# A memory-attention and GEGLU kernel: probabilities kept in two tiles, G evicted ahead of a nested addition, nested pieces in another order

## The chip, the cores and the metric

The kernel runs on one core of one Trainium2 chip. The metric is the device time of one execution in microseconds; what is given for a kernel is the median of its runs. Matmuls run on TensorE (PE; its weight loads are shown as PEld), the other work on VectorE (DVE), ScalarE (ACT) and GpSimd (POOL), and DMAs are issued by SyncE (SP).

## The reference

One sequence of 2048 rows, width 576, goes through two branches, and a sigmoid gate mixes them:

```python
q, k, v = x @ wq, x @ wk, x @ wv          # 32 heads of 18, 4 segments of 512 rows
for s in range(4):                        # per head
    p = softmax(qs @ ks.T * 18**-0.5 + causal_mask)
    a_dot = p @ vs
    a_mem = (phi(qs) @ M) / (phi(qs) @ z + 1e-6)     # phi(t) = t + 1 if t > 0 else exp(t)
    o = sigmoid(beta) * a_mem + (1 - sigmoid(beta)) * a_dot
    M, z = M + phi(ks).T @ vs, z + sum(phi(ks))
a = o @ wo
b = (gelu(x @ w_gate) * (x @ w_up)) @ w_down         # width 4608 inside
out = g * a + (1 - g) * b                 # g = sigmoid(sum(x * gate_w))
```

All is float32. The kernel keeps each matmul operand as two 16-bit words, a high one (the rounded value) and a low one (what the rounding left), and takes three products for one: high by high, high by low, low by high. A pair is made in two instructions: ScalarE copies to 16 bits, and Pool or VectorE subtracts.

## The kernel before

The program has three parts. First the four segments are projected (`project`, `put_columns`, `put_rows`), with the memory M and its recall; the loop runs over segments s and eight tiles j, and small pieces of other work are hung in by `beside_rows`, `behind_rows`, `beside_products`. Then come 72 steps `step(v)` of the inner width: v is split into f, p (block of 128 inner columns, half of the rows) and into fb, i4 (pair of blocks, place within it). Each makes two outputs of 128 inner columns by 512 rows twice (gate and up), in a scheme with fewer products than the plain one (Strassen's kind): sums of x and sums of weights are formed ahead, and three banks of the matmuls' memory, G (`X`), U (`Y`) and V, gather the products. The products of V are themselves nested one level deeper for half of the steps: `nest(at, n)` with n from 0 to 3 runs in the steps with i4 == 3 and i4 == 0, for the step behind, and piece 4 at the start of that step. Between the pieces VectorE copies or adds half a bank (`hold`, 256 columns). At the end VectorE multiplies gate and up (`hidden`), ScalarE and Pool make the pair (`hidden_pair`), and the down-projection of a block that is done runs as `chains` of `down` pieces, six matmuls of 288 columns in a "dn" bank each, which VectorE adds to `acc`. The third part is the output projection.

Attention lies inside the steps. With LAG 4, step v handles head index k = v - 4, a head of one half of the rows, in two units a = 2k and 2k + 1 (one segment each). For a unit, `scores` issues four matmuls (128, 256, 384 and 512 columns); `piece(qi)` lets VectorE add the mask, write the piece to the tile pf and find its maxima; `powers` has ScalarE form the bound mb and four exponentials; `pair_rows` makes the pairs of 768 and 512 columns (ScalarE's copy to ph, L1136, Pool's subtraction into pf itself, L1137); `turn_rows` turns ph and pf by DMA (L1142) into pt; `values` multiplies pt with the values. The tile pf has two buffers. The banks of the pieces are "st" (two) and "dn" (two, shared with the down-projection) and "pv".

The order of the work is written by hand: in `step` each engine takes its instructions in the order of the calls, and nothing is reordered. What is hung in where is decided by lines like these, near the start of a step and at its end:

```python
            weights_nest(fb, i4, 0)
...
            if on(k - 1):
                powers(2 * k - 1)
                pair_rows(2 * k - 1, 0)
                pair_rows(2 * k - 1, 1)
                turn_rows(2 * k - 1)
...
            nest(at, 3)
            ends.append((f, e, Y, g1))
```

`weights_nest` and `weights_first` scale, sum and pair the next blocks' weights (`nest_pairs`, L375 on ScalarE and L377 on Pool; `nest_sums`, L384 to L387 on Pool; `low_g`, L342). `scale_g` (L304, VectorE) scales a block of raw weights. `result_low` (L1186, VectorE) makes the low words of an attention result once in four steps.

Of the kernel before, what the change touches and what calls it, by code (L numbers as in the profile page):

```python
# [13 lines left out]
OP = mybir.AluOpType  # L14
# [29 lines left out]
def kernel(ctx: ExitStack, tc: tile.TileContext, xs, wqk, wv, wo, wgu, wd, beta, out):  # L44
# [475 lines left out]

    first, stay = ExitStack(), ctx.enter_context(ExitStack())
    with tc.tile_pool(name="prj", bufs=2, side="right", reuse_waits="tile") as pp:
# [45 lines left out]
        def make_v(k):  # L568
            t = W[9 + k] = pa.tile([P, 2, D + 2], F16, name="wv", bufs=5)
            pair_of(t, raw_v[:, k], wsc[:, 1:2])  # L570
# [186 lines left out]
        with tc.manual_schedule(engines=ORDERED):  # L757
# [96 lines left out]
            def beside_rows(s, q):  # L854
# [14 lines left out]
                if s == 3 and q == 1:  # L869
                    scales(0)  # L870
                    scales_out(0)
                    scale_g(0)
                    scale_g(1)

            def behind_rows(s, q):
                if s == 3:
                    if q < 3:
                        form_sums(1, q, -1, pool if q == 0 else dve)
                    if q == 0:
                        squares(0, 0, 0, act_square)  # L880
                    if q == 3:
                        rescale_words(2)
                        high_g(0, 0)
                        low_g(0, 0)

            def beside_products(s, j):
                if 0 < s < 3 and j == XJ[s]:
                    scale_x(s + 1)
                if s == 0:
# [31 lines left out]
                    if 3 <= j < 6:  # L921
                        finish_later()
                    if 1 <= j < 6:
                        make_v(j - 1)
                    if j == XJ[0]:
                        norm_x(0, bank("V"))
                        scale_x(1)
# [110 lines left out]
            put_columns(*done)  # L1038
            recall(3, 3)
            finish_later()  # L1040
# [10 lines left out]
    with tc.tile_pool(name="keep", bufs=2, side="right", reuse_waits="tile") as kp, ExitStack() as tail:  # L1051
# [3 lines left out]
        pairs16, turned_p, pvb = {}, {}, {}  # L1055
# [40 lines left out]
        COL = [0, P, 3 * P, 6 * P, 10 * P]  # L1096

        PIECES = ((3, 0, "st", "st"), (2, 64, "st", "st"), (1, 64, "dn", "dn"), (0, 0, "pv", "dn"))

        def scores(a):  # L1100
# [4 lines left out]
            prob[a] = ap_.tile([P, 10 * P], F32, name="pf", bufs=2)  # L1105
# [6 lines left out]
            def piece(qi):  # L1112
                dve.tensor_tensor_reduce(prob[a][:, COL[qi] : COL[qi + 1]], out[qi], mask[:, L - (qi + 1) * P :],  # L1113
# [4 lines left out]
        def powers(a):  # L1118

            p = prob[a]  # L1120
            b = ap_.tile([P, 4], F32, name="mb", bufs=2)
            c = 2 * (a // (2 * H)) + a % 2
            act.activation(b, mx.pop(a), AF.Copy, bias=LN256, scale=esc[:, 1, c : c + 1])  # L1123
            for qi in (1, 0, 2, 3):
                r = p[:, COL[qi] : COL[qi + 1]]
                act.activation(r, r, AF.Exp, bias=b[:, qi : qi + 1], scale=esc[:, 0, c : c + 1])  # L1126

        def pair_rows(a, i):

            p = prob[a]  # L1130
            if i == 0:
                pairs16[a] = ap_.tile([P, 10 * P], F16, name="ph", bufs=2)
                turned_p[a] = ap_.tile([P, 20, P], F16, name="pt", bufs=2)
            h = pairs16[a]
            cols = (slice(0, 6 * P), slice(6 * P, 10 * P))[i]
            act.activation(h[:, cols], p[:, cols], AF.Copy)  # L1136
            pool.tensor_tensor(p.bitcast(F16)[:, cols], p[:, cols], h[:, cols], OP.subtract)  # L1137

        def turn_rows(a):
            t = turned_p[a]  # L1140
            for i, h in enumerate((pairs16.pop(a), prob.pop(a).bitcast(F16)[:, : 10 * P])):
                sp.dma_start(t[:, 10 * i : 10 * i + 10], h, transpose=True)  # L1142
# [94 lines left out]
        def gl_tile():  # L1237
            return mp2.tile([P, L], F32, name="gl", bufs=3)

        def product(o, f, a, x, h, l, start=False):  # L1240

            w = pair_g[f]
            for k in range(2):
                for i, b in ((0, h), (0, l), (1, h)):
                    pe.matmul(o, w[:, i, (a + k) * P : (a + k + 1) * P], x[:, b + k],  # L1245
                              start=start and k == 0 and i == 0 and b == h, stop=k == 1 and i == 1,
                              skip_group_check=True)

# [69 lines left out]
        ahead = {}  # L1318

        def first_product(v):  # L1320
            f, p = divmod(v, 2)
            V = bank("V")
            w = flat(s3_first["t"])
            for k, b in ((0, X00), (1, X10)):
                for i, j in ((0, 0), (0, 1), (1, 0)):
                    a = (4 * i + 2 * f + k) * P
                    x = nest_x(p)[j][:, b * HX : (b + 2) * HX]
                    pe.matmul(V, w[:, a : a + P], x, start=k == i == j == 0, stop=k == i == 1, skip_group_check=True)
            if v == 3:
                s3_first.pop("t")  # L1330
                hh_free.append(s3_first.pop("slot"))
            g1 = gl_tile()
            dve.tensor_copy(g1, V)
            return V, g1

# [8 lines left out]
        def nest(at, n):  # L1344
# [24 lines left out]
            if n == 4:  # L1369
                nest_product(b, A, WS4, X11, p)  # L1370

        ends, puts = [], {}

        def end_pair():

            for g in ends:
                hidden(*g)
                if g is ends[0]:
# [3 lines left out]
            for f, c, o, g in ends:  # L1382
# [3 lines left out]
        def step(v):  # L1386
# [22 lines left out]
            elif i4 < 2:  # L1409
                if on(k - 2):  # L1410
                    values(2 * k - 3)
                nest((fb, p), 4)
                V, g1 = nested.pop((fb, p)), gl_tile()
                dve.tensor_copy(g1, V)
# [5 lines left out]
            put(2 * k - 1, 3)  # L1420
            dve.tensor_copy(Y, X)
            if v == 0:
                last_sum(1, 1)
                nest_sums_x(0)
            if v == 1:
                nest_sums_x(1)
            if v in (2, 3):
                for i in range(2):
                    nest_pairs_x(v - 2, i)
# [381 lines left out]
```

## Time and profile before

| | |
|---|---|
| median of 3 runs | 1620.98 us (1614.13 to 1621.68) |
| profiled execution | 1622.97 us |
| its span, from the first to the last instruction | 1621.3 us |
| mean granted TensorE clock | 0.996 |
| TensorE busy, 0 to 219 us (projections) | 211.75 us |
| TensorE busy, 219 to 290 us (first steps) | 66.00 us, clock 0.95 |
| TensorE busy, 290 to 1500 us (steps with attention) | 1182.66 of 1210 us |
| TensorE busy, 1500 to 1622 us (the tail) | 116.93 us |

In the rows of a timeline the first number is the start in us from the span's start, the second the time of the merged instructions, then engine, line, operation, output<-inputs, shapes and count; brackets give how long the engine sat idle before, and who released it. In rows of waits stand the total in us, the number of times and the longest. In a row of a window stand its bounds, its length, the busy time and instruction count of PE, PEld, DVE, ACT and POOL, the granted clock, the DMA share and GB/s. Ends of matmuls are modelled, so idle times on TensorE are a little less than the distance between starts shows.

### The profile page before, as it was taken

How to read it: one execution, taken by the hardware profiler on the slowest of the kernel's cores; microseconds unless marked ns; L12 is line 12 of the kernel's file. 1: busy time of each engine (PE TensorE's matmuls, PEld its weight loads, DVE VectorE, ACT ScalarE, POOL GpSimd, SP SyncE). 2: the span in 40 equal slices, each digit the busy share in tenths (PEclk: the TensorE clock that was granted, in tenths of full speed). 3: DMA queues.
4: the chain of work that ended last, by engine and by line, in shares of the span. 5: the costliest groups of instructions: out<-in, count | busy, mean ns of one | idle time of the engine just before them, and what ended most of it. 6: DMA issues, size and time to landing. Idle time of an engine off the chain costs nothing. (4 is left out here: it accounts for less than half of the span.)

```text
span 1621.3 us, 34060 instructions
## 1 busy us (share of the span) xinstructions
PE 1577.3 (97%) x12220; PEld 962.6 (59%) x12220; DVE 1272.2 (78%) x3256; ACT 1180.6 (73%) x2057; POOL 1119.6 (69%) x1218
## 2 busy tenths in 40 slices
PE   9999998999999999999999999999999989999999
PEld 5665654565556655555566565556555555656577
DVE  6779884878788878878787887788888878887665
ACT  7466543879788888878887877888888878786421
POOL 4245556677686867686867767686858676876597
PEclk9999999999999999999999999999999999999999
DMA  6533331567786787877777777778787878764546
GB/s 225 205 121 112 129 129 57 105 122 127 121 140 127 125 136 139 128 134 122 132 130 130 130 126 121 134 128 136 135 142 134 127 126 130 137 120 91 110 85 172
DMA packets 472834, 209.98 MB, mean 130 GB/s; under 512 B 427688, under 2 KB 437416, under 8 KB 472152
## 3 DMA queue, kind: packets, MB, share of 16 engines
q1 hardware_dynamic: 472664, 207.80, 66.3%
q8 instruction: 96, 1.57, 0.4%
q14 instruction: 74, 0.61, 0.1%
HBM read 91.87 MB, written 27.26 MB: 73 GB/s over the span
## 5 line engine op out<-in xcount | busy, mean ns | idle before, releaser
L1137 POOL TENSOR_TENSOR pf<-pf,ph 128x768 f16<-128x768 f32 (+1 forms) x256 | 366.5, 1432 | 305.4 <-ACT ph L1136 295.2
L1245 PEld LDWEIGHTS <-pairg 128*128 128x128 f16 x2592 | 251.3, 99 | 266.2 <-issue 26.9
L1203 PE MATMUL dn<-paird,hhr 128*128 128x288 f16 x2124 | 327.8, 287 | 6.8 <-DVE mx L1113 6.7
L1211 DVE SCALAR_TENSOR_TENSOR acc<-dn,ev,acc 128x288 f32<-128x288 f32 x534 | 271.4, 514 | 44.0 <-PE dn L1203 35.6
L1126 ACT ACTIVATE pf<-pf,mb,esc 128x256 f32<-128x256 f32 (+3 forms) x512 | 292.9, 642 | 5.5 <-issue 0.4
L1203 PEld LDWEIGHTS <-hhr 128*128 128x128 f16 x2160 | 207.3, 98 | 101.5 <-issue 20.9
L1245 PE MATMUL G<-x,pairg 128*128 128x512 f16 x864 | 211.2, 381 | 5.5 <-DVE gl L1226 5.5
L1245 PE MATMUL U<-xt,pairg 128*128 128x512 f16 x864 | 210.0, 379 | 1.6 <-DVE gl L1471 1.6
L1203 PE MATMUL dn<-paird,hhd 128*128 128x288 f16 x1272 | 205.3, 287 | 5.7 <-DVE mx L1113 5.7
L1136 ACT ACTIVATE ph<-pf 128x768 f16<-128x768 f32 (+1 forms) x256 | 172.4, 720 | 0.0
L342 POOL TENSOR_TENSOR pairg<-raw,pairg 128x384 f16<-128x384 f32 (+2 forms) x144 | 158.2, 1120 | 15.5 <-ACT pairg L338 15.5
L1203 PEld LDWEIGHTS <-hhd 128*128 128x128 f16 x1296 | 124.9, 98 | 58.1 <-issue 12.7
L1113 DVE CUSTOM_DVE_ANT_0 pf<-st,mask 128x512 f32<-128x512 f32 (+1 forms) x256 | 157.2, 614 | 0.0
L1113 DVE CUSTOM_DVE_ANT_0 pf<-dn,mask 128x256 f32<-128x256 f32 (+1 forms) x192 | 67.2, 375 | 99.1 <-PE dn L1110 61.8
L1123 ACT ACTIVATE mb<-mx,esc 128x4 f32<-128x4 f32 x128 | 37.1, 290 | 120.9 <-DVE mx L1113 120.8
L1235 ACT ACTIVATE gl<-gl,sc 128x512 f32<-128x512 f32 x110 | 75.2, 713 | 56.8 <-DVE gl L1498 40.8
L1341 PE MATMUL V<-xt,nest 128*128 128x256 f16 x714 | 106.4, 273 | 8.5 <-DVE hold L1368 3.7
L1245 PE MATMUL U<-x,pairg 128*128 128x512 f16 x432 | 106.2, 383 | 0.8 <-DVE gl L1498 0.8
L1245 PE MATMUL V<-x,pairg 128*128 128x512 f16 x432 | 106.5, 383 | 0.0
L1232 POOL TENSOR_TENSOR hhr<-gl,hhr 128x512 f16<-128x512 f32 x67 | 80.9, 1217 | 19.5 <-ACT hhr L1231 18.2
L1341 PEld LDWEIGHTS <-nest 128*128 128x128 f16 x714 | 66.5, 97 | 42.1 <-issue 24.5
L1156 PE MATMUL pv<-vt,pt 128*128 128x37 f16 x2560 | 85.2, 179 | 3.9 <-DMA pt<-pf 3.9
(355 smaller groups left out, 3128.5 us busy)
## 6 DMA issues: line engine op xcount, KB each, us to landing
raw<-in_wgu_dram SPq DMA_DIRECT2D x36, 640.0 KB
rawd<-in_wd_dram SPq DMA_DIRECT2D x36, 288.0 KB
qt<-qk SPq DMA_DIRECT2D x132, 72.0 KB
kt<-qk SPq DMA_DIRECT2D x132, 72.0 KB
qk<-stage SPq DMA_DIRECT2D x36, 256.0 KB
qt<-qk SPq DMA_DIRECT2D x132, 36.0 KB
kt<-qk SPq DMA_DIRECT2D x132, 36.0 KB
vp<-vstage SPq DMA_DIRECT2D x16, 296.0 KB
```

What stands on the lines that cost most here:

```text
L342: pool.tensor_tensor(spot(f, *p, 1), raw_g[f][:, p[0] : p[1]], spot(f, *p, 0), OP.subtract)
L1113: dve.tensor_tensor_reduce(prob[a][:, COL[qi] : COL[qi + 1]], out[qi], mask[:, L - (qi + 1) * P :], 1.0, -3e38, OP.add, OP.max, mx[a][:, q ...
L1126: act.activation(r, r, AF.Exp, bias=b[:, qi : qi + 1], scale=esc[:, 0, c : c + 1])
L1136: act.activation(h[:, cols], p[:, cols], AF.Copy)
L1137: pool.tensor_tensor(p.bitcast(F16)[:, cols], p[:, cols], h[:, cols], OP.subtract)
L1156: pe.matmul(ov, pr[:, 10 * i + COL[qi] // P + kb], v[:, 4 * e + kb, c0 : c0 + VC], start=kb == 0 and i == 0, stop=kb == qi and i == 1)
L1203: pe.matmul(o[:, :NH], hh[:, a, q * P : (q + 1) * P], w[:, b, n * NH : (n + 1) * NH], start=i == 0, stop=i == 5)
L1211: dve.scalar_tensor_tensor(av, o[:, :NH], ev, av, OP.mult, OP.add)
L1232: pool.tensor_tensor(hh[:, 1], t, hh[:, 0], OP.subtract)
L1235: act.activation(t, o, AF.Gelu_apprx_tanh, scale=scl[f // 2][0][:, 2 + c : 3 + c])
L1245: pe.matmul(o, w[:, i, (a + k) * P : (a + k + 1) * P], x[:, b + k], start=start and k == 0 and i == 0 and b == h, stop=k == 1 and i == 1, ...
L1341: pe.matmul(o, w[:, (7 * c + i) * P : (7 * c + i + 1) * P], x[d], start=start and n == 0, stop=n == 2, skip_group_check=True)
```

## The change

The tile pf is split in two: pb23 holds the pieces of 384 and 512 columns, pb01 those of 128 and 256. `pair_rows` and `turn_rows` are merged into `powers`; the pairs have 896 and 384 columns, and the low words of both go into pb23:

```diff
-        COL = [0, P, 3 * P, 6 * P, 10 * P]
+        COL = {2: 0, 3: 3 * P, 0: 7 * P, 1: 8 * P}
+        SPLIT = 7 * P
...
+            big = ap_.tile([P, SPLIT], F32, name="pb23", bufs=2)
+            prob[a] = big, ap_.tile([P, 10 * P - SPLIT], F32, name="pb01", bufs=2)
...
+            low = prob[a][0].bitcast(F16)
+            for i, (p, cols) in enumerate(zip(prob[a], (slice(0, SPLIT), slice(SPLIT, 10 * P)))):
+                for qi in ((3, 2), (1, 0))[i]:
+                    r = scored(a, qi)
+                    act.activation(r, r, AF.Exp, bias=b[:, qi : qi + 1], scale=esc[:, 0, c : c + 1])
+                act.activation(h[:, cols], p, AF.Copy)
+                pool.tensor_tensor(low[:, cols], p, h[:, cols], OP.subtract)
+            prob.pop(a)
+            for i, r in enumerate((h, low[:, : 10 * P])):
+                sp.dma_start(t[:, 10 * i : 10 * i + 10], r, transpose=True)
```

In a step, G is evicted by `hidden` before nested piece 3's addition (`end_first`), piece 4 (`nest_last`) comes behind product X, the copies of V and of G come ahead of a score piece, and `powers` of the odd unit comes ahead of `weights_nest`:

```diff
+            if fb and i4 < 2:
+                nest_last(fb, V, p)
+                dve.tensor_copy(g1, V)
+                dve.tensor_copy(Y, X)
+                put(2 * k - 1, 3)
...
-            weights_nest(fb, i4, 0)
...
             if on(k - 1):
                 powers(2 * k - 1)
-                pair_rows(2 * k - 1, 0)
-                pair_rows(2 * k - 1, 1)
-                turn_rows(2 * k - 1)
+            weights_nest(fb, i4, 0)
...
-            some(fb - 1, early[3:4])
+            some(fb - 1, early[3:])
             put(2 * k, 3)
-            some(fb - 1, early[4:])
...
+            if on(k - 1):
+                values(2 * k - 2)
+            if v != 3:
+                nest(at, 2)
             if low is not None:
                 result_low(low)
-            if on(k - 1):
-                values(2 * k - 2)
             if fb:
                 low_rests(f, (X, U4, x1), (Y, UG, x2_))
                 ends.append((f, c, X, g0))
+                if at:
+                    end_first()
```

In the first block, the nested pieces of v == 3 stand between its products and no longer in one run, `first_product(3)` uses the bank "pv", and some sums and scalings of x and of weights come later:

```diff
+            if v == 3:
+                nest(at, 0)
             some(fb - 1, early[0 if v == 4 else 1 : 2])
...
+            if v == 3:
+                nest(at, 1)
             some(fb - 1, early[2:3])
...
+            if v == 3:
+                nest(at, 2)
...
-            if v == 2:
-                scale_g(3, FRONT)
```

In the projections, `make_v(3)` and `make_v(4)` form their pairs on ScalarE and Pool, `scale_g(0)` and `scale_g(1)` are called from `behind_rows` and no longer from `beside_rows`, and segment 0 takes its `norm_x` and `scale_x` at another place:

```diff
+            if k < 3:
+                pair_of(t, r, sc)
+                return
+            act.activation(r, r, AF.Copy, scale=sc)
+            act.activation(t[:, 0], r, AF.Copy)
+            pool.tensor_tensor(t[:, 1], r, t[:, 0], OP.subtract)
...
-                    scale_g(0)
-                    scale_g(1)
...
+                    if 0 < q < 3:
+                        scale_g(q - 1)
```

On Pool, in a step with i4 == 3 (hhd is the pair of a hidden block, nest the pairs of nested weights), the rows before:

```order
L1232 TENSOR_TENSOR hhd_6038<-gl,hhd_6038 128x512
L1232 TENSOR_TENSOR hhd_6041<-hold_5091,hhd_6041 128x512
L377 TENSOR_TENSOR nest<-nest 128x256
L377 TENSOR_TENSOR nest<-raw,nest 128x256
L1137 TENSOR_TENSOR pf<-pf,ph 128x768
L1137 TENSOR_TENSOR pf<-pf,ph 128x512
L342 TENSOR_TENSOR pairg<-raw,pairg 128x384
```

On Pool at the same place the rows of the changed kernel, where L1266 and L1173 are what L1232 and L1137 were:

```order
L1266 TENSOR_TENSOR hhd_6062<-gl,hhd_6062 128x512
L1266 TENSOR_TENSOR hhd_6065<-hold_5108,hhd_6065 128x512
L1173 TENSOR_TENSOR pb_6028<-pb_6028,ph 128x896
L1173 TENSOR_TENSOR pb_6028<-pb_6029,ph 128x384
L377 TENSOR_TENSOR nest<-nest 128x256
L377 TENSOR_TENSOR nest<-raw,nest 128x256
L342 TENSOR_TENSOR pairg<-raw,pairg 128x384
```

The two subtractions of the probabilities have moved ahead of the low words of two nested weights. ScalarE's instructions for the same unit and weights have moved in the same way.

On VectorE, at the end of a step with i4 == 3 and the start of the one behind it (pieces of the scores are ISA rows with mx), the rows before:

```order
L1365 TENSOR_TENSOR hold_6207<-V,hold_6207 128x256
L1186 SCALAR_TENSOR_TENSOR ob<-ob,wsc,oh 128x576
L1368 TENSOR_TENSOR hold_6207<-V,hold_6207 128x256
L1226 SCALAR_TENSOR_TENSOR gl<-G,sc,gl 128x512
L1113 ISA pf,mx<-dn,mask 128x256
L1113 ISA mx 128x1
L1113 ISA pf,mx<-dn,mask 128x128
L1113 ISA mx 128x1
L1226 SCALAR_TENSOR_TENSOR hold_5368<-U,sc,hold_5368 128x512
L1414 COPY gl<-V 128x512
L1113 ISA pf,mx<-st,mask 128x512
```

On VectorE at the same place the rows of the changed kernel, where L1260 is what L1226 was and L1372 what L1368 was:

```order
L1369 TENSOR_TENSOR hold_6232<-V,hold_6232 128x256
L1220 SCALAR_TENSOR_TENSOR ob<-ob,wsc,oh 128x576
L1260 SCALAR_TENSOR_TENSOR gl<-G,sc,gl 128x512
L1372 TENSOR_TENSOR hold_6232<-V,hold_6232 128x256
L1155 ISA pb_6320,mx<-dn,mask 128x256
L1155 ISA mx 128x1
L1155 ISA pb_6320,mx<-dn,mask 128x128
L1155 ISA mx 128x1
L1260 SCALAR_TENSOR_TENSOR hold_5387<-U,sc,hold_5387 128x512
L1430 COPY gl<-V 128x512
L1431 COPY U<-G 128x512
L1155 ISA pb_6319,mx<-st,mask 128x512
```

The eviction of G stands one row earlier, and the copy of G stands ahead of the piece of 512 columns.

More of the change, by code (lines that the diff above doesn't have):

```diff
@@ L886, in beside_products @@
             def beside_products(s, j):
-                if 0 < s < 3 and j == XJ[s]:
+                if s < 3 and j == XJ[s]:
+                    if s == 0:
+                        norm_x(0, bank("V"))
                     scale_x(s + 1)
@@ L1038 @@
             put_columns(*done)
+            finish_later()
             recall(3, 3)
+            ahead[0] = first_product(0)
             finish_later()
@@ L1235, in gelu @@
             act.activation(t, o, AF.Gelu_apprx_tanh, scale=scl[f // 2][0][:, 2 + c : 3 + c])
[L1237 to L1247, printed above, removed]
         def rest(o, f, a, x, parts=(0, 1)):
@@ L1316, in act_squares @@
                 squares(b, f, i, act_square)
[L1318 to L1334, printed above, removed]
         nested, holds = {}, {}
@@ L1381, in end_pair @@
                             puts[max(puts)](qi)
-            for f, c, o, g in ends:
+            for f, c, o, g, *_ in ends:
                 hidden_pair(f, c, g)
@@ L1427, in step @@
             if v in (2, 3):
-                for i in range(2):
-                    nest_pairs_x(v - 2, i)
+                nest_pairs_x(v - 2, 0)
             if v == 1:
```

99 lines of the change are left out of this document (56 added, 43 removed).

## The prediction

> **What bounds the kernel now.** I read the page first, then the waits of TensorE, then the busy time of the stretches, then single places in time. The page says that TensorE is the bound:
>
> ```profile
> span 1621.3 us, 34060 instructions
> PE 1577.3 (97%) x12220; PEld 962.6 (59%) x12220; DVE 1272.2 (78%) x3256; ACT 1180.6 (73%) x2057; POOL 1119.6 (69%) x1218
> ```
>
> TensorE does the same matmuls after the change, so the change can only act on the 44 us in which it isn't busy, and on stretches in which its clock is halved. The view of TensorE's waits says whom it waited for (total us, times, longest):
>
> ```profile
> PE dn L1203 <- DVE mx L1113: 12.3, 11, 2.8
> PE G L1245 <- DVE gl L1226: 5.5, 31, 0.4
> PE pv L1156 <- DMA pt<-pf: 3.9, 3, 1.5
> PE V L1341 <- DVE hold L1368: 3.7, 9, 0.5
> PE dn L419 <- DVE wv L115: 2.4, 1, 2.4
> PE U L717 <- DVE vstage L634: 1.7, 1, 1.7
> PE U L1245 <- DVE gl L1471: 1.6, 1, 1.6
> ```
>
> The first row is a down-projection (L1203) that needs a "dn" bank, which VectorE frees only when it has read a score piece out of it (L1113). Why VectorE is late stands in the view of the line that turns the probabilities (L1142, the transposing DMAs), among those who waited for it, and in the timeline of the longest case on TensorE:
>
> ```profile
>   DVE pf L1113: 27.0, 12
> ```
> ```profile
> 994.93 0.53 PE L1203 MATMUL dn<-paird,hhd 128*128 128x288 f16 x3
> 998.26 0.53 PE L1203 MATMUL dn<-paird,hhr 128*128 128x288 f16 x3 [2.80 <-DVE mx L1113]
> 998.99 2.65 PE L1245 MATMUL U<-x,pairg 128*128 128x512 f16 x6
> ```
>
> So 12 times a score piece couldn't be written into pf because the transposes of two units earlier were still reading it, 27.0 us of VectorE's time, of which 12.3 came through to TensorE. The idle time counts from a modelled end. Groups of three L1203 start 0.37 us apart where nothing waits, so the second group was due at 995.30 and lost 2.96, 0.16 more than the row says. The third row shows a second price: six L1245 matmuls took 2.65 us. The windows show the granted clock (the third figure from the end, after POOL's) at three such places:
>
> ```profile
> 45.90:49.40 3.50, 3.50 (x12) 1.30 (x12) 2.21 (x8) 1.58 (x3) 1.28 (x5) 0.63 0.86 304
> 267.80:274.60 6.80, 5.77 (x21) 2.45 (x20) 3.25 (x6) 0.63 (x1) 1.31 (x2) 0.56 0.17 52
> 998.30:1001.70 3.40, 3.40 (x13) 1.52 (x13) 2.78 (x8) 1.33 (x2) 3.24 (x5) 0.62 0.56 110
> ```
>
> Lost there, by length times what is missing of the clock: 3.50 x 0.37 = 1.3, 6.80 x 0.44 = 3.0, 3.40 x 0.38 = 1.3 us.
>
> **The change part by part.** The sum is made against the profiled execution, 1622.97 us (the span of 1621.3 and 1.7 around it), which lies 2.0 above the median of the three runs shown (1620.98).
>
> *The probabilities in two tiles.* The pieces of 256 and 128 columns come first on VectorE and hold "dn" and "pv". They now go to a tile of their own (pb01). Its last readers are ScalarE's copy and Pool's subtraction; the transposes read only pb23, so the piece that still waits for them is the one of 512 columns. On VectorE these two stand here:
>
> ```profile
> 486.77 0.42 DVE L1113 CUSTOM_DVE_ANT_0 pf<-dn,mask 128x256 f32<-128x256 f32 x1 [1.69 <-PE dn L1110]
> 488.95 0.68 DVE L1113 CUSTOM_DVE_ANT_0 pf<-st,mask 128x512 f32<-128x512 f32 x1
> ```
>
> That gives 2.18 us of grace. The 12 waits of 27.0 us are 2.25 each in the mean, so nearly all is covered; the largest leave some tenths, and behind that piece waits a "st" bank that TensorE wants only later. Gain: 12.3 + 11 x 0.16 = 14.1, with the half-clock stretch 1.3, together 15.4; I take **-15** (bounds -12 and -16).
>
> [...]
>
> *The nested pieces.* In 31 steps TensorE runs nested products through one bank V, waiting for VectorE between them. One step (TensorE, then VectorE):
>
> ```profile
> 492.38 0.53 PE L1203 MATMUL dn<-paird,hhr 128*128 128x288 f16 x3
> 492.98 0.81 PE L1341 MATMUL V<-xt,nest 128*128 128x256 f16 x6
> ...
> 496.22 0.49 PE L1341 MATMUL V<-xt,nest 128*128 128x256 f16 x3 [0.40 <-DVE hold L1368]
> 496.88 1.46 PE L1245 MATMUL G<-x,pairg 128*128 128x512 f16 x6 [0.17 <-DVE gl L1226]
> ```
> ```profile
> 494.18 1.65 DVE L1186 SCALAR_TENSOR_TENSOR ob<-ob,wsc,oh 128x576 f16<-128x576 f32 x1
> 495.75 0.41 DVE L1368 TENSOR_TENSOR hold<-V,hold 128x256 f32<-128x256 f32 x1
> ```
>
> Between 492.38 and 492.98 lie 0.60 for a group that needs 0.37: 0.23 lost, which the idle view doesn't name. Piece 4 (496.22) loses 0.40 and 0.16. Product G, due after three matmuls of 256 columns (0.107 each, from six in 0.65), starts 0.66 after it: 0.34 lost. So a step loses 0.5 to 1.1 us, some 0.85 in the mean, 26 us in 31 steps. After the change G is evicted first, product G comes before piece 4, and the copy of V ahead of that of G. In steps with i4 == 0 the wait for G goes; what is left is about 0.1 on the nested addition and about 0.2 on product V, which now waits for the later copy out of V: I estimate 0.45 gained in 15 or 16 steps, 7 us. In steps with i4 == 3 the result's low words (L1186, 1.65 us) still stand ahead of the eviction, so G's start only trades its wait for that of piece 4: nothing. Sum **-7** (bounds -20, if all but 0.2 a step goes, and +2).
>
> *Pool's order in i4 == 3.* The powers of the odd unit, with Pool's two subtractions, are moved ahead of the low words of two nested weights (L377), which TensorE needs for nested piece 0:
>
> ```profile
> 468.74 2.88 POOL L1137 TENSOR_TENSOR pf<-pf,ph 128x768 f16<-128x768 f32 x2 [0.67 <-ACT ph L1136]
> ...
> 487.53 0.68 POOL L377 TENSOR_TENSOR nest<-nest 128x256 f16<-128x256 f32 x1
> 488.29 0.67 POOL L377 TENSOR_TENSOR nest<-raw,nest 128x256 f16<-128x256 f32 x1
> 489.11 2.88 POOL L1137 TENSOR_TENSOR pf<-pf,ph 128x768 f16<-128x768 f32 x2 [0.15 <-ACT ph L1136]
> ```
> ```profile
> 489.55 0.82 PE L1341 MATMUL V<-xt,nest 128*128 128x256 f16 x6
> ```
>
> The first L377 ended at 488.21; TensorE reads these low words with the sixth matmul, 0.54 after 489.55, so the slack is 1.88. Two subtractions cost 2.8 to 2.9. But Pool's chain, full from 468.74 on, began with 0.67 of waiting for ScalarE's copy; that copy comes earlier now, since two exponentials stand ahead of it and no longer four. 2.85 - 0.67 - 1.88 = 0.3 late, with some tenths for copies that gate less evenly: 0.4 in 16 steps, **+6** (0 to +15, the latter if the chain isn't drawn in). Who waits is TensorE, with all down-projections behind it.
>
> *Values that wait for transposes* (3.9 in three, third row of the waits). ScalarE's queue made them late:
>
> ```profile
> 484.31 0.42 ACT L375 ACTIVATE nest<-nest 128x256 f16<-128x256 f32 x1 [3.00 <-POOL nest L385]
> 485.38 0.42 ACT L375 ACTIVATE nest<-raw 128x256 f16<-128x256 f32 x1 [0.65 <-POOL raw L387]
> ```
>
> The powers (L1123 and L1126), which stood behind these two rows, now stand ahead of them and can begin some 4 us earlier (3.00 + 0.42 + 0.65 + 0.3); the subtractions follow on Pool 1.4 us earlier (two L377 fewer ahead). The waits were at most 1.5: **-3.5** (-4.4, with 3 x 0.16 of modelled ends, to +3, if ScalarE's conversion for L377 comes late in turn and the next piece waits for it some 0.2 a step).
>
> *The first block.* The wait of 1.6 for L1471 goes with the scaling that is put behind it; the halved clock came from one run of nested pieces with nothing between, which are now spread. But the first piece is early, and its low words are not:
>
> ```profile
> 262.27 0.66 POOL L377 TENSOR_TENSOR nest<-nest 128x256 f16<-128x256 f32 x1
> ```
> ```profile
> 264.71 0.82 PE L1341 MATMUL V<-xt,nest 128*128 128x256 f16 x6
> ...
> 270.15 0.80 PE L1341 MATMUL V<-xt,nest 128*128 128x256 f16 x3 [0.52 <-DVE hold L1368]
> ```
>
> Pool was at work without a break from 246.72 to 263.7; by the order, piece 0 reaches TensorE at about 257, and its words come at 261 to 263. I expect a new stall of 4 to 5 us with some half clock (1.3 to 3.0 by the rows above, I take 2.1). Against it stand the 1.6, the 3.0, and from 264.71 to 270.15 5.4 us for 18 matmuls that need 1.9, so 3.5 of small waits: 4.5 + 2.1 - 8.1 = **-1.5** (-6 if the stall is 2.6 and halves no clock, +3 if it is 5.6 with twice 3.0).
>
> *Stage 0.* Two of VectorE's paired weights go to ScalarE and Pool. The row is that of a subtraction of nearly the same size on Pool:
>
> ```profile
> 473.81 1.28 POOL L399 TENSOR_TENSOR paird<-rawd,paird 128x576 f16<-128x576 f32 x1
> ```
>
> The wait of 2.4 (fifth row of the waits) shrinks to some 1.2, since Pool's subtraction then ends last, and with the wait the half clock (1.3) goes: **-2.5** (-3.9 to +2).
>
> *Stage 3.* Two scalings on VectorE stand ahead of the eviction that TensorE waited for. They move behind it, and the wait of 1.7 in the sixth row goes: **-1.7** (-1.9 with the 0.16 of the modelled end, to 0). The other moves (sums of x to the end of the first step, a copy of V now on the path of stage 3's end) lie under TensorE's work at places without a wait: 0, or 1 us each if that cover is thin.
>
> Sum: -15 - 7 + 6 - 3.5 - 1.5 - 2.5 - 1.7 = -25.2. 1622.97 - 25.2 = 1597.8 for a profiled execution, less 2.0 for the median: **1595.8 us**, which I round to 1595.5.
>
> **The rivals.** About 8 us (0.5%) is what a measurement of this kernel can tell from no change: faster is under 1612.9, slower over 1629.1.
>
> *Pool becomes the bound (slower).* Pool's times stretch beside VectorE, as the rows show:
>
> ```profile
> 258.19 2.13 POOL L1232 TENSOR_TENSOR hhd<-gl,hhd 128x512 f16<-128x512 f32 x1
> 485.30 1.16 POOL L1232 TENSOR_TENSOR hhd<-gl,hhd 128x512 f16<-128x512 f32 x1
> ```
>
> The same subtraction took 1.84 times as long. If that met both subtractions ahead of the nested low words, these would be 2.85 x 1.84 - 0.67 - 1.88 = 2.7 late in 16 steps, 43 us for my 6: 1595.5 + 37 = 1632.5. It decides from some 2.5 us per step. Against it: in this place the pair took 2.88 (489.11), as at 468.74. Chance 0.05. The milder form, the chain not drawn in, is 15 for 6: 1604.5, chance 0.14.
>
> [...]
>
> *The DMA wait only changes its place.* If the transposes land later by 1.3 us, as Pool's second subtraction could make them, the 512 piece waits in each of the 12 cases and holds "st" and everything behind it on VectorE: 12 x 1.2 = 14 back, 1609.5. For it: VectorE works in order. Against it: the 2.18 of grace and Pool's chain that comes earlier. Chance 0.09.
>
> *The nested waits all go* (-20 for -7) and Pool is in time (0 for +6): 1576.5. For it: the order removes each wait by name. Chance 0.10.
>
> **How the numbers follow.** Forecast 0.62, with 1584 to 1607 as its own spread from the bounds of the unknown terms (chiefly nested -20 to +2, Pool 0 to +15, first block -6 to +3). With the milder Pool case and the displaced wait inside, and the best case at the edge, the range is **1578 to 1612**; outside lie the bad Pool case (0.05), half of the best one (0.05) and those 0.09 that the next sentence names. The forecast, the milder Pool case, the displaced wait and the best case are faster and have 0.95; of these 0.09 is where the milder Pool case or the displaced wait meets the bad ends of other terms, 0.08 within 0.5% and 0.01 slower. So faster 0.86, same 0.08, slower 0.06 with the bad Pool case.
>
> **What would show it.** Right: no TensorE wait for a score piece of over 0.5 us; the transposes' waiters on VectorE only at the 512 piece; no wait of values on a transpose; no half clock at 46 and 998; nested piece 0 in i4 == 3 waiting for Pool by under 0.6; a stall of 4 to 5 us near 257. Wrong: TensorE waiting for Pool's nested words by over 1 us a step; "st" waits in the place of the "dn" ones; or the two-tile part giving under 10.

## The result, and the profile after

The changed kernel takes 1605.38 us in the median of four runs (1603.99 to 1606.29), the kernel before 1620.74 in four: the ratio is 0.9913, with a 95% interval of 0.9886 to 0.994. That is 14 us faster (10 to 18), where 25 were forecast. The profiled execution, 1603.99 us, lies 19.0 below that of before (1622.97). The page and TensorE's waits of the changed kernel (total us, times, longest):

```profile
span 1602.3 us, 33969 instructions
PE 1568.8 (98%) x12220; PEld 953.8 (60%) x12220; DVE 1271.0 (79%) x3254; ACT 1208.5 (75%) x2059; POOL 1117.8 (70%) x1220
```
```profile
PE V L1345 <- POOL nest L377: 12.2, 17, 4.9
PE G L529 <- DVE gl L1260: 6.3, 17, 0.4
PE dn L94 <- ACT nest L89: 3.2, 15, 0.2
...
PE dn L419 <- POOL wv L606: 0.8, 1, 0.8
...
PE dn L1237 <- DVE mx L1155: 0.3, 1, 0.3
```

The largest row of before (12.3 for a score piece) is down to 0.3, and the waits of values on pt, of stage 0 and of stage 3 are gone or small. At the top stand a row that was forecast, but smaller (Pool's nested words), the eviction of G, which has 17 cases left of 31, and a row that before didn't have at all: L94, a small product that adds up the squares of the next weights, waits for ScalarE.

Idle times of this view count from modelled ends. A second reckoning is used below: the distance between the starts of two neighbouring matmuls, less what the first takes where nothing waits (0.216 us for 512 columns, the distance at which they start in the trace of before; others in proportion). The figures are good to 0.1. By this reckoning, summed over the steps from 290 to 1505 us, with the rows by line:

| | before | changed | e1: two tiles alone |
|---|---|---|---|
| down-projection for a score piece | 14.8 (14) | 0.5 (1) | 1.0 (1) |
| values for a transpose | 4.4 (3) | 0 | 0 |
| product G for its eviction | 10.0 (30) | 8.7 (16) | 11.7 (34) |
| nested pieces for VectorE, with small gaps among them | 19.0 | 3.5 | 16.3 |
| product V for its copy (L1430) | 0 | 6.7 (32) | 0 |
| nested piece 0 for Pool | 0 | 9.9 (16) | 0 |
| L94 for ScalarE, and the gap behind it | 0 | 7.6 (15) | 0 |

Here is one step with i4 == 3 of the changed kernel, on Pool and on TensorE:

```profile
479.60 2.89 POOL L1173 TENSOR_TENSOR pb<-pb,ph 128x896 f16<-128x896 f32 x2
482.44 0.67 POOL L377 TENSOR_TENSOR nest<-nest 128x256 f16<-128x256 f32 x1
```
```profile
481.98 0.71 PE L1345 MATMUL V<-xt,nest 128*128 128x256 f16 x5
483.17 0.28 PE L1345 MATMUL V<-xt,nest 128*128 128x256 f16 x1 [0.48 <-POOL nest L377]
```

Five of the six matmuls ran; the sixth, which reads the low words, was due at 482.53 and started at 483.17, when Pool had come through the two subtractions: 0.64.

And the small product L94 in a step with i4 == 1: ScalarE's last square and TensorE's rows, changed and before (in each pair ScalarE first):

```profile
365.59 0.19 ACT L89 ACTIVATION_READ_ACCUMULATOR nest<-rawd 128x1 f32 x1
```
```profile
364.73 0.90 PE L1237 MATMUL dn<-paird,hhd 128*128 128x288 f16 x6
365.83 0.39 PE L94 MATMUL dn<-stat,ones 128*128 128x10 f32 x2 [0.21 <-ACT nest L89]
```
```profile
371.76 0.19 ACT L89 ACTIVATION_READ_ACCUMULATOR nest<-rawd 128x1 f32 x1
```
```profile
371.69 0.90 PE L1203 MATMUL dn<-paird,hhd 128*128 128x288 f16 x6
372.42 0.29 PE L94 MATMUL dn<-stat,ones 128*128 128x10 f32 x2
```

Before, ScalarE was done at 371.95, 0.47 ahead of the product. Now it is done at 365.78 and the product stands waiting for it.

In the first block the forecast stall is there, and halves the clock behind it (0.59, the third figure from the end):

```profile
251.80 0.39 PE L1345 MATMUL V<-xt,nest 128*128 128x256 f16 x2 [0.60 <-ACT nest L375]
257.12 0.40 PE L1345 MATMUL V<-xt,nest 128*128 128x256 f16 x1 [4.93 <-POOL nest L377]
```
```profile
257.10:260.60 3.50, 3.48 (x12) 1.49 (x13) 0.42 (x1) 0.00 (x0) 0.67 (x1) 0.59 0.47 136
```

### The profile page after: what moved, and what is told of

It reads as the page before. It is cut to its first block, busy times and chain, and to the rows that moved or that the text cites. A ratio compares the mean times of both kernels' runs of the same rounds, so it can differ in the third digit from the quotient of the medians.

```text
span 1602.3 us, 33969 instructions
## 1 busy us (share of the span) xinstructions
PE 1568.8 (98%) x12220; PEld 953.8 (60%) x12220; DVE 1271.0 (79%) x3254; ACT 1208.5 (75%) x2059; POOL 1117.8 (70%) x1220
## 5 line engine op out<-in xcount | busy, mean ns | idle before, releaser
L1173 POOL TENSOR_TENSOR pb<-pb,ph 128x896 f16<-128x896 f32 (+1 forms) x256 | 368.6, 1440 | 295.7 <-ACT ph L1172 285.6
L1171 ACT ACTIVATE pb<-pb,mb,esc 128x512 f32<-128x512 f32 (+3 forms) x512 | 305.0, 642 | 5.3
L1245 DVE SCALAR_TENSOR_TENSOR acc<-dn,ev,acc 128x288 f32<-128x288 f32 x534 | 265.9, 513 | 42.3 <-PE dn L1237 34.4
L1172 ACT ACTIVATE ph<-pb 128x896 f16<-128x896 f32 (+1 forms) x256 | 188.5, 736 | 8.1
L1155 DVE CUSTOM_DVE_ANT_0 pb<-st,mask 128x512 f32<-128x512 f32 (+1 forms) x256 | 157.0, 613 | 0.0
L1155 DVE CUSTOM_DVE_ANT_0 pb<-dn,mask 128x256 f32<-128x256 f32 (+1 forms) x192 | 67.1, 374 | 78.2 <-PE dn L1152 78.2
L1345 PE MATMUL V<-xt,nest 128*128 128x256 f16 x714 | 109.1, 273 | 13.1 <-POOL nest L377 12.2
L1345 PEld LDWEIGHTS <-nest 128*128 128x128 f16 x714 | 64.4, 97 | 50.0 <-POOL nest L377 16.9
L1190 PEld LDWEIGHTS <-pt 128*128 128x128 f16 x2560 | 83.4, 96 | 5.5
L1266 POOL TENSOR_TENSOR hhr<-gl,hhr 128x512 f16<-128x512 f32 x67 | 78.6, 1183 | 11.5 <-ACT hhr L1265 11.5
```

Of the source, the lines that this page charges most:

```text
L1155: dve.tensor_tensor_reduce(scored(a, qi), out[qi], mask[:, L - (qi + 1) * P :], 1.0, -3e38, OP.add, OP.max, mx[a][:, qi : qi + 1])
L1172: act.activation(h[:, cols], p, AF.Copy)
L1173: pool.tensor_tensor(low[:, cols], p, h[:, cols], OP.subtract)
L1190: pe.matmul(ov, pr[:, 10 * i + COL[qi] // P + kb], v[:, 4 * e + kb, c0 : c0 + VC], start=kb == 0 and i == 0, stop=kb == qi and i == 1)
L1245: dve.scalar_tensor_tensor(av, o[:, :NH], ev, av, OP.mult, OP.add)
L1266: pool.tensor_tensor(hh[:, 1], t, hh[:, 0], OP.subtract)
```

## Where the gain went: the theory and its rivals

The theory after the result: the gain in the steps is that of the two tiles. Beside e1 in the table, the new order in the steps gains 9 us of nested waits and loses 17.5: 9.9 at Pool's nested words (the moved powers) and 7.6 at L94 (ScalarE's powers take longer, and TensorE comes sooner). Work moved in the projections gives some of that back. The rivals: that the earlier powers and not the tiles took the DMA waits away; that L94's wait belongs to the place of that product; that the longer powers are a matter of the pieces' sizes. Eleven edited kernels and the changed one once more were run. Times taken on different occasions can be compared for kernels with two tiles, as e10 shows for the changed kernel; the kernel before moves from run to run, 1611 to 1622.

**e1, the two tiles alone.** To the kernel before the two tiles are added, with the new order of ScalarE's exponentials and copies that goes with them; the rest of the order stays. A part of the edit:

```diff
-            prob[a] = ap_.tile([P, 10 * P], F32, name="pf", bufs=2)
+            big = ap_.tile([P, SPLIT], F32, name="pb23", bufs=2)
+            prob[a] = big, ap_.tile([P, 10 * P - SPLIT], F32, name="pb01", bufs=2)
...
+                for qi in ((3, 2), (1, 0))[i]:
```

> The kernel before with the two tiles (and the order of exponentials and copies that goes with them) alone. Theory: the score pieces of 256 and 128 columns no longer wait for transposes, so TensorE's waits for a score piece (12.3 us in 11) fall under 1.5 us, and the half-clock stretch at 998 is gone; ScalarE's exponentials and copies take 0.28 us longer a unit, as in the changed kernel, since each copy now stands right behind the exponential that it reads. Time 1604 to 1611, that is 10 to 16 below the kernel before. Rival (the gain came from Pool's and ScalarE's earlier powers, which let the transposes land earlier, and not from the tiles): the waits stay at 8 us or more, time 1615 to 1622.

Measured: 1600.07 us, before 1615.49, ratio 0.9902 (0.9876 to 0.9927). TensorE's waits in it:

```profile
PE G L1244 <- DVE gl L1225: 6.0, 34, 0.4
PE dn L419 <- DVE wv L115: 2.4, 1, 2.4
...
PE dn L1202 <- DVE mx L1120: 0.8, 1, 0.8
```

The DMA waits are gone with no powers moved; that it is the tiles and not ScalarE's new order is left to e2. The kernel is even 5 us faster than the changed one, so all other edits together cost time. The time was below the expected band: the waits of values on pt (4.4 in the table) went as well, and the kernel before stood at 1615 beside it and not at the 1621 from which the band was drawn.

**e2, one tile again.** The changed kernel, with

```diff
-            big = ap_.tile([P, SPLIT], F32, name="pb23", bufs=2)
-            prob[a] = big, ap_.tile([P, 10 * P - SPLIT], F32, name="pb01", bufs=2)
+            big = ap_.tile([P, 10 * P], F32, name="pf", bufs=2)
+            prob[a] = big[:, :SPLIT], big[:, SPLIT:]
```

> The changed kernel with both tiles put back into one of 1280 columns, all else as changed. Theory: the waits of the first score pieces for the transposes are back, 8 to 15 us of TensorE's time, time 1613 to 1622. Rival (the new order alone would have been enough, since the transposes now land earlier): waits under 3 us, time 1604 to 1608.

Measured: 1612.13 us (1608.24 to 1616.42), ratio 0.9976 (0.9961 to 0.9992).

```profile
PE dn L1237 <- DVE mx L1155: 9.0, 12, 2.4
```
```profile
  DVE pf L1155: 16.9, 7
```

The second row is from the view of the transposing DMAs: VectorE waits for them again, 16.9 us in 7 score pieces. The waits come back under the new order, so the tiles and not the order removed them. The spread comes back too: in each set of runs the one-tile kernels range over 7 to 10 us (4 to 19 runs), the two-tile kernels over 0.3 to 2.7 (4 to 10 runs). The median is just under the expected band, 6.8 above the changed kernel and not the 15 of the profile of before. A part of the waits costs nothing here, since the wait for Pool's nested words falls from 12.2 to 9.0; presumably Pool catches up while TensorE waits for a score piece.

**e3, Pool's low words first.** In steps with i4 == 3 the changed kernel's Pool makes the nested low words ahead of the subtractions; ScalarE's order stays:

```diff
+            if on(k - 1) and i4 == 3:
+                powers(2 * k - 1, lambda: weights_nest(fb, i4, 0))
```

> The changed kernel; in steps with i4 == 3 Pool makes the low words of the two nested weights ahead of the two subtractions of the probabilities, ScalarE's order stays. Theory: TensorE's wait for Pool's nested words (0.63 in 16 steps, 12.2 us with the first block's 4.9) falls to the first block's alone; 1605 - 10 = 1595 (1593 to 1598). The probabilities' low words come 1.3 us later on Pool and the values still don't wait for them. Rival (the late transposes take the wait over): waits of values on pt of 4 us or more, time 1599 to 1605.

Measured: 1598.0 us, ratio 0.989 (0.9868 to 0.9912).

```profile
PE V L1350 <- POOL nest L377: 4.9, 1, 4.9
PE pv L1195 <- DMA pt<-pb: 4.0, 4, 1.1
```

Only the first block's wait for Pool is left; 7.4 us are gained of the 10 expected. The rest went where the rival had it: four units of values now wait for transposes (1.1 at most), whose subtractions Pool reaches later by two L377 of 0.67.

**e4, the sum of squares later.** The changed kernel, with

```diff
-            if v == 0 or fb > 1 and i4 == 1:
+            if v == 0:
...
             some(fb - 1, early[2:3])
+            if fb > 1 and i4 == 1:
+                scales(fb + 1)
+                scales_out(fb + 1)
```

> The changed kernel; in steps with i4 == 1 the small product that sums the squares of the next weights (L94) comes one stretch of products later. Theory: that wait is ScalarE being 0.3 us late, so 2 us of other products in front of it hide it all: the row of L94 (3.2 us in 15 by the view, 5.7 from start to start) vanishes, 1605 - 5.5 = 1600 (1598 to 1602). Rival (the start-to-start gap is mostly the small product's own weight load, which stays wherever it stands): the time falls by under 2, 1603 to 1606.

Measured: 1614.38 us, 9 slower, where 5 faster were expected: a miss. L94 has no row any more, but

```profile
PE dn L1237 <- DVE mx L1155: 14.4, 16, 0.9
```

`scales` takes six small instructions on VectorE, and the move put them right ahead of the score piece that frees a "dn" bank. On VectorE and Pool:

```profile
519.95 1.89 DVE L266 TENSOR_SCALAR z<-x,z 128x4 f32<-128x4 f32 x1
...
522.83 0.41 DVE L1155 CUSTOM_DVE_ANT_0 pb<-dn,mask 128x256 f32<-128x256 f32 x1
```
```profile
519.93 2.88 POOL L1173 TENSOR_TENSOR pb<-pb,ph 128x896 f16<-128x896 f32 x2 [0.22 <-ACT ph L1172]
```

An instruction on four columns took 1.89, from the start of Pool's subtraction on. In the changed kernel this line took 0.23 to 0.65, in 19 cases. I had reckoned with the place of the product on TensorE and left out the queue of VectorE behind it.

**e5, copies behind the exponentials.** The changed kernel, with

```diff
-                for qi in ((3, 2), (1, 0))[i]:
+            for qi in (3, 2, 1, 0):
                     act.activation(r, r, AF.Exp, bias=b[:, qi : qi + 1], scale=esc[:, 0, c : c + 1])
+            for p, cols in zip(prob[a], (slice(0, SPLIT), slice(SPLIT, 10 * P))):
                 act.activation(h[:, cols], p, AF.Copy)
```

> The changed kernel; ScalarE makes all four exponentials of a unit first and the copies of 896 and 384 columns behind them, so that no copy stands right behind the exponential that it reads. Theory: the 0.28 us that ScalarE takes longer for a unit than before is the lost overlap of two such pairs; the powers of a unit go from 4.09 back to 3.8 or 3.85 (mb to the next instruction), the sums of squares end 0.3 earlier, and the wait of L94 (3.2 in 15) falls under 0.8. Pool's first subtraction of a unit can start up to 0.9 later, so the wait for Pool's nested words may grow from 0.63 a step to as much as 1.5; time 1598 to 1614, read from the rows. Rival (the longer time is that of the other sizes, 896 and 384): 4.09 stays, L94's wait stays at 3.

Measured: 1608.62 us, ratio 0.9962 (0.9949 to 0.9975). ScalarE's powers of a unit, in the changed kernel and in e5:

```profile
474.24 1.41 ACT L1171 ACTIVATE pb<-pb,mb,esc 128x512 f32<-128x512 f32 x2
475.69 0.95 ACT L1172 ACTIVATE ph<-pb 128x896 f16<-128x896 f32 x1
476.55 0.97 ACT L1171 ACTIVATE pb<-pb,mb,esc 128x256 f32<-128x256 f32 x2
477.55 0.52 ACT L1172 ACTIVATE ph<-pb 128x384 f16<-128x384 f32 x1
477.98 0.40 ACT L375 ACTIVATE nest<-nest 128x256 f16<-128x256 f32 x1
```
```profile
475.76 2.29 ACT L1170 ACTIVATE pb<-pb,mb,esc 128x512 f32<-128x512 f32 x4
477.95 1.35 ACT L1172 ACTIVATE ph<-pb 128x896 f16<-128x896 f32 x2
479.20 0.40 ACT L375 ACTIVATE nest<-nest 128x256 f16<-128x256 f32 x1
```
```profile
PE V L1345 <- POOL nest L377: 20.3, 17, 4.9
```

From the first exponential to the instruction behind the last copy it is 3.74 in the one and 3.44 in the other, with the same sizes, so the 0.3 is a matter of order: the copy right behind the exponential that it reads starts 0.04 after its end (475.69), where the exponential behind that copy starts 0.09 ahead of the copy's end (476.55). L94's row is gone. Pool's first subtraction can start later, and its row grew by 8: as expected, the one loss against the other.

**e6, the result's low words behind.** The changed kernel, with

```diff
-            if low is not None:
-                result_low(low)
             if fb:
...
             nest(at, 3)
+            if low is not None:
+                result_low(low)
```

> The changed kernel; the result's low words (L1220, in steps with i4 == 3) come behind the eviction of G and the addition of nested piece 3. Theory: they alone made the eviction late, so product G's wait (0.54 from start to start in 16 steps, 6.3 us in 17 by the view) goes: 1605.4 - 8 = 1597.5 (1595 to 1600). Rival (VectorE is simply full there, and the next thing behind, the score pieces that free the dn banks, is late in turn): a wait for L1155 of 5 us or more, time 1602 to 1607.

Measured: 1599.45 us, ratio 0.9908 (0.9887 to 0.9929). The wait of G falls to 0.6, but

```profile
PE V L529 <- DVE gl L1430: 4.0, 16, 0.8
```

The copy out of V, which stands further back in VectorE's queue, is now what TensorE comes to too early: 6 us are gained of 8.

**e7, the first block's pieces one place later.** The changed kernel, with nested pieces 0, 1 and 2 of v == 3 each one place further:

```diff
-            if v == 3:
-                nest(at, 0)
             some(fb - 1, early[0 if v == 4 else 1 : 2])
...
             if v == 3:
-                nest(at, 1)
+                nest(at, 0)
```

> The changed kernel; in the first block (v == 3) nested pieces 0, 1 and 2 come one place later each. Theory: the stall of 4.9 us at 252 is piece 0 ahead of Pool's words, which are there at 257; one place later it starts at about 256.5, and the stall and the half-clock stretch behind it (1.4 us) go, with up to 1.5 of small waits of the pieces that stand closer: 1605.4 - 5 = 1600.5 (1599 to 1603). Rival (Pool is late for whatever comes next, the same time is lost at product U or G of the next step): 1604 to 1606.

Measured: 1603.2 us, ratio 0.9931 (0.9913 to 0.9949): 2 gained of 5. A place is 1.6 us of products, not the 5 that I had taken for it:

```profile
257.03 0.39 PE L1345 MATMUL V<-xt,nest 128*128 128x256 f16 x1 [4.00 <-POOL nest L377]
```

**e8, e3, e6 and e7 together.** 

> The changed kernel with Pool's nested low words ahead of the subtractions, the result's low words behind the eviction of G, and the first block's pieces one place later. Theory: the three act at different places and add up: 1598.0 - 8 - 5 = 1585 (1582 to 1589), 30 below the kernel before. Rival (they share the same slack, since Pool's chain and VectorE's run through all steps): 1590 to 1596.

Measured: 1592.04 us, ratio 0.9861 (0.9842 to 0.9879), where 1582 to 1589 were expected. From 1605.4 the three gained 7.4, 5.9 and 2.2 alone, 15.5 in all; together 13.3. At the sizes measured they nearly add up, but the time lies in the band of the rival, shared slack; where the 2.2 went was not traced.

**e9, four together.** e8 with e5's order on ScalarE, and in the first block

```diff
                 high_g(2, 1)
-                low_g(2, 1)
...
                 weights_nest(fb, i4, 0)
+            if v == 3:
+                low_g(2, 1)
```

> The kernel of e8 with two more edits: ScalarE's copies behind all four exponentials, and in the first block Pool's low words of block 2's second part behind those of the nested weights (3.0 us of Pool that stood ahead of them). Theory: the sums of squares end 0.28 earlier, so L94's wait (2.7 in 13) is under 0.5 in all, worth 4 to 5; the first block's stall of 4.0 falls to about 1.2 and its half clock goes, worth 3 to 4: 1592.0 - 8 = 1584 (1581 to 1587). Rival (Pool's later subtractions make the values wait for their transposes, 4.4 in 5 in e8, in twice as many units): 1587 to 1592.

Measured: 1585.57 us, ratio 0.9814 (0.9791 to 0.9837), the fastest of all. What TensorE still waits for:

```profile
PE pv L1195 <- DMA pt<-pb: 3.8, 4, 1.4
PE V L529 <- DVE gl L1434: 3.1, 12, 0.8
PE V L1350 <- POOL nest L377: 2.0, 1, 2.0
```

L94 has no row, the first block's stall is 2.0 and halves no clock (1.00 from 250 to 260.6 us), and the values wait no more than in e8.

**e10, the changed kernel again.** 

> The changed kernel itself once more, beside the other kernels of this call. Theory: nothing in it waits for a transpose, so it repeats within 0.15% wherever it runs, 1603 to 1607, while the kernel before moves with the landing of its transposes, 1611 to 1622 between calls. Rival (the chips differ as wholes): it moves with the kernel before.

Measured: 1604.95 us (1604.08 to 1605.64) beside a kernel before of 1613.09 (1611.34 to 1620.28), ratio 0.9934 (0.991 to 0.9958). It repeats to 0.03%, while the kernel before is 8 us below its first median.

**e11, tiles and nested order.** e1 with `end_first`, `nest_last`, the copies of V and G ahead of the score piece, and the order of values and pieces that goes with them:

```diff
+            if fb and i4 < 2:
+                nest_last(fb, V, p)
+                dve.tensor_copy(g1, V)
+                dve.tensor_copy(Y, X)
+                put(2 * k - 1, 3)
...
+                if at:
+                    end_first()
```

> The kernel of e1 (the two tiles alone) with the nested order alone added: G evicted first, piece 4 behind product X, the copies of V and G ahead of the score piece. Theory: the nested waits of the steps with attention fall from 24.7 (start to start) to 19, but TensorE comes to L94 half a us sooner than ScalarE's squares, whose margin in e1 is 0.08: a wait of about 0.4 in 15 steps is new and gives the gain back; 1598 to 1601 against the 1600.1 of e1. Rival (L94's wait comes from the powers that were moved): no row of L94, 1593 to 1596.

Measured: 1600.16 us, ratio 0.9906 (0.9878 to 0.9935), against 1600.07 of e1.

```profile
PE pv L1155 <- DMA pt<-pb: 3.3, 4, 1.5
PE dn L94 <- ACT nest L89: 3.2, 15, 0.2
```

From start to start the nested rows and G fall from 27.9 in e1 to 17.3, 10.6 gained; L94 with the gap behind it takes 7.6, the values 4.0. So the nested order is worth nothing by itself, and L94's wait comes from it, on a margin that the longer powers had already taken, as e1's rows show (ScalarE, then TensorE; the square is done at 371.50, the product in front of L94 runs until about 371.7):

```profile
371.31 0.19 ACT L89 ACTIVATION_READ_ACCUMULATOR nest<-rawd 128x1 f32 x1
```
```profile
370.96 0.90 PE L1202 MATMUL dn<-paird,hhd 128*128 128x288 f16 x6
371.70 0.29 PE L94 MATMUL dn<-stat,ones 128*128 128x10 f32 x2
```

The margin is 0.47 before, 0.20 here; the 0.28 between them is what ScalarE's powers take longer.

**e12, tiles and moved powers.** e1 with

```diff
-            weights_nest(fb, i4, 0)
...
             if on(k - 1):
                 powers(2 * k - 1)
+            weights_nest(fb, i4, 0)
```

> The kernel of e1 with the powers of the odd unit ahead of the nested weights alone added. Theory: Pool's nested words come late by 0.6 in each of 16 steps as in the changed kernel, a row V <- POOL nest of 7 to 10 us, and no row of L94: 1600.1 + 9 = 1609 (1607 to 1611). Rival (without the earlier start of TensorE's steps Pool is in time): under 2 us in that row, 1599 to 1602.

Measured: 1609.23 us, ratio 0.9969 (0.9955 to 0.9983), 9 above e1.

```profile
PE V L1340 <- POOL nest L377: 7.7, 16, 0.5
```

That edit alone costs what it costs in the changed kernel, and it has no row of L94.

## Why the prediction was right, and where its sizes were off

The direction and the range (1578 to 1612) held, and the mechanism of the largest term. But the direction is owed to that term alone: all other terms together were forecast to gain 10.2, and the changed kernel is 5.3 slower than e1, which has the tiles without them. Their sum came out with the wrong sign, and the range held because it was wide. The gain was 14 and not 25; the parts one by one:

- *Two tiles, -15.* Right: 14.8 to 0.5 from start to start, and e1 alone gives a ratio of 0.9902. But the size belongs to one execution. The profile of before (1622.97) was a bad draw: in four sets of runs the kernel before had medians of 1613 to 1621, and beside the three lower ones the changed kernel gains 8 to 10 us and not 14. By e2 the tiles are worth 6.8 under the new order, which is under the 10 that the prediction gave as a sign of being wrong; by e1 they are worth 15. "Less 2.0 for the median" was too little a correction for a term that depends on when transposes land (one of ph took 1.28 to 4.42 us in the trace of before).
- *Nested pieces, -7.* The waits of G, V and the pieces fell by 10, more than forecast; the forecast 0.2 for product V is there (6.7 in 32), and the low words (L1220) hold the eviction in i4 == 3 as said (0.54 in 16; e6). What failed is the end of the path: I didn't ask what TensorE meets next when it comes half a us sooner. It meets L94, and the gain is given back there (e11).
- *Pool's order, +6.* The wait is that of the forecast (e3, e12), the size 9.9. The step that was mis-sized is "- 0.67", the waiting for ScalarE's copy that was to go. Counted from the unit's first exponential, Pool's chain does begin 0.62 earlier (2.47 us behind it for 3.09: 458.37 to 460.84, before 465.65 to 468.74). But the unit ahead of it takes 0.28 longer on ScalarE, for the reason in e5, so some 0.34 are left, and 2.85 - 0.34 - 1.88 = 0.63, where 0.64 was measured.
- *Other moves, 0.* Here the sum lacked a term: ScalarE's new order was counted as the same work in another order. It takes 0.28 more a unit by the rows (1208.5 us busy for 1180.6 in all), which took 0.28 of the 0.47 that covered L94; e5 shows it. By itself that costs nothing (e12 has no row of L94); with TensorE half a us sooner it does (e11). "Name the work that hides it" was done for Pool and VectorE, not for ScalarE.
- *Values, -3.5.* The size came: no row is left (4.4 from start to start). That the earlier powers did it is not shown: in e1 and e12 the row is gone as well, and in e1 the powers weren't moved. In e3, e8, e9 and e11, where subtractions come later than in the changed kernel, rows of 3.3 to 4.4 are back; e1 and e5 have later subtractions too and no such row, so that alone doesn't decide it.
- *First block -1.5, stage 0 -2.5, stage 3 -1.7.* Together -5.7. By the start of the same matmuls in both traces the changed kernel is 2.7 ahead at 77 us, 6.3 ahead at 212 us and 6.3 at 277 us: the projections gave 6.3 where 4.2 were forecast, the first block nothing where 1.5 were; that the sum of the three fits is luck. The stall there is 4.9 with one half-clock stretch, as described.
- *The rivals.* The bad Pool case didn't come, its milder form did in part (9.9 of 15). The displaced DMA wait didn't: no line of the changed trace has VectorE waiting for a transpose. In the two rows that the bad case rests on, VectorE was busy for 2.10 of the 2.13 us and for 0.00 of the 1.16; that this stretched the one was the author's estimate from these two. In the changed kernel the first of the two subtractions takes 1.89 in the mean of 128. Which stalls had half clock behind them, and which had not, stands at the end.

What stays open: why the transposes land late in some units and runs and not in others, and with it which kernels' values wait. No run here varied the DMA traffic.

## What to carry to other kernels

When a tile is written by one engine and read by a slow transfer (here transposes of 1.3 to 4.4 us), give the piece that holds a scarce bank a tile of its own; here it took nearly all of the wait and most of the spread between runs. When a wait is removed on the bounding engine, look for the next thing that engine meets and compute its margin, on every engine: here 0.47 us of cover on ScalarE was worth 7.6 us. And price a term that depends on the landing of transfers over several runs, not from one profile.

## What the runs showed of the hardware

- ScalarE's copy right behind the exponential that it reads started 0.04 us after that one's end, where the exponential right behind that copy started 0.09 ahead of the copy's end. The same six instructions took 3.74 us with two such pairs (the changed kernel, from 474.24 on) and 3.44 with none (e5, from 475.76 on).
- A VectorE instruction on 128x4 elements took 1.89 us (e4, at 519.95), from the start of a Pool subtraction that takes 1.89 in the mean of the changed kernel, where the same line took 0.23 with nothing on Pool beside it (row below, from the timeline of before in stage 3).

```profile
168.01 0.23 DVE L266 TENSOR_SCALAR z<-x,z 128x4 f32<-128x4 f32 x1
```

- TensorE's granted clock was halved behind stalls of 2.44 and 2.80 us in before (0.50 in the windows 46.78:50.20 and 999.10:1002.51) and of 4.93 in the changed kernel (0.59 in 257.10:260.60). Behind one of 4.00 in e7 six 512-column matmuls took 2.56 us from 257.22 on, where six ahead of it took 1.30 from 249.30 on. The clock was not halved behind the stall of 2.00 in e9 (1.00 in 257.10:260.60), nor in before behind two waits for a score piece, 2.09 until 714.34 and 2.73 until 1301.31 (1.00 in 711:719 and 1297:1306). So the length of a stall alone doesn't decide it: 2.73 halved nothing where 2.44 did; e1 has the same wait as before at L419 (2.4) and a clock of 1.00 over 0 to 219 us, where before has 0.99; and the half clock of the first steps in before (0.50 in 268.65:275.47) stands behind waits of 0.98 at most. What does decide it, no run here shows. The rows of before around the stall of 2.44 (TensorE's busy time is the figure behind the length):

```profile
43.37:46.78 3.41, 0.97 (x6) 0.48 (x5) 3.41 (x5) 0.00 (x0) 1.26 (x1) 1.00 0.88 248
46.78:50.20 3.42, 3.42 (x9) 1.18 (x8) 2.13 (x7) 2.35 (x4) 2.08 (x5) 0.50 0.89 357
```

The second of them, at half clock with TensorE busy, lost 1.7 us by length times what is missing of the clock (3.42 x 0.50). The prediction's windows at 45.90 and 998.30 began 0.9 and 0.8 ahead of the half clock and gave 1.3.
